# Attention with two MLP layers on one core: earlier weight conversions and an earlier x split in the first batch

## The chip, the cores and the metric

The kernel runs on one core of one Trainium2 chip. The metric is the device time of one execution in microseconds (us); lower is better. The engines are PE (TensorE, matmuls and transposes), DVE (VectorE), ACT (ScalarE) and POOL (GpSimd). SP issues nearly all DMAs of this kernel, from a queue that works in order.

## The reference

Attention over 4 batches, 8 heads, 576 positions and a head dimension of 64, with a threshold below each row's maximum, and after it two MLP layers (512 to 2048 to 512) with different activations. All in float32:

```python
scores = (q @ k.T) / sqrt(64)
scores = where(scores >= max(scores) - tau, scores, -1e9)
attn = exp(scores - max(scores)); attn = attn / (sum(attn) + 1e-9)
x = (attn @ v), heads side by side          # 2304 x 512
h = x @ w_in1
g = where(h >= 1, h, where(h <= -1, 0, (h + 1)**2 / 4))
x = g @ w_out1
h = x @ w_in2
out = (h * clip(h + 3, 0, 6) / 6) @ w_out2
```

## The kernel before, in words

**Attention.** The heads are taken two at a time: 16 jobs, four to a batch. A job has five blocks of query rows (four of 128, one of 64). Each block computes scores on PE (line 335), which DVE copies out of PSUM with the row maxima (line 348); ACT takes the exponent (line 360), DVE applies the threshold and sums (lines 363 and 369), PE transposes the result (line 284), ACT copies it out (lines 397 to 415), and PE multiplies by v (line 433). From job 4 on, q and k come in strips of 32 columns (line 227, from SP), and DVE transposes them (lines 293 and 309). When a job is done, its rows are divided by their sums: for most jobs POOL multiplies with factors that take a way through DRAM (lines 452 to 488); in the last job of the first batch PE transposes the factors and DVE multiplies (lines 496 to 507).

`attention()` is a generator that writes the blocks out one after the other, with the blocks' counter `t` from 0 (`mode["t"]` counts from 1). What has to happen beside a block is entered in `plan` by `at(t, what, j)`: "q" and "k" load and turn the next job, "z", "f" and "n" are the steps of the division. Job j's "n" stands at t = 5j + 9.

**First layer.** As soon as the four jobs of batch 0 are done, `dense1` starts on its rows, in groups of 256 columns, and runs between the blocks of the later jobs (PE lines 676 and 738). Every float32 operand is taken apart into a rounded part and the rest, and a product is made of three matmuls. `split_x` does this for x, in four pieces of 128 rows, one to a job (`kk`): ACT writes the rounded part (line 656), DVE the rest (line 657). Where x is still in SBUF (`here`), the pieces are read from there.

**Weights.** They are converted item by item, 512 KB each, in two halves. `split_a` has lines 118 and 121 on ACT, 122 on POOL, 129 on DVE; `split_b` has 135 on DVE, 137 on POOL, 139 on ACT and 141 on POOL. Five raw buffers stand in turn; after each second half the next load is issued from SP (lines 96 and 99). During the first batch halves are written by the loop at the end of the program, at most one to a block, until FIRST = 5 items are converted; after that `pace` writes them by the progress of `dense1`.

**Order.** The instructions are reordered when the program is built: an instruction that is ready may be put ahead of where it is written. `after(...)` holds some in place: the ACT lines 118 and 139 come behind the last exponent that was written before them, and in `split_x` line 656 behind the last exponent, line 657 behind the last mask.

Of the kernel before, what the change touches and what calls it, by code (L numbers as in the profile page):

```python
# [18 lines left out]
def kernel(  # L19
# [17 lines left out]
    KD = DM // 128  # L37
# [33 lines left out]
    def narrow(t, g):  # L71
        return t[g // 2][:, :, (g % 2) * GRP:(g % 2 + 1) * GRP]

    def f32(ap):
        return ap.bitcast(F32)
# [109 lines left out]
    weights = Weights()  # L185
# [5 lines left out]
    NBLK = 5  # L191
# [15 lines left out]
    mode = {"mlp": False, "att": True, "step": False, "t": 0, "s": 0, "n": 0}  # L207
# [233 lines left out]
    def pv_run(n):  # L441
        for _ in range(min(n, len(pvq))):
            pv_chunk()
# [68 lines left out]
    def attention():  # L512

        order = [(j, i) for j in range(NJ) for i in range(NBLK)]
        n = len(order)
        turns, tailq, maskq = [], [], []
        plan = {}

        def at(t, what, *x):
            plan.setdefault((t, what), []).append(x)  # L520

        for j in range(NJ):
            at(NBLK * j + (4 if j < HP - 1 else 3), "q", j + 1)
            at(NBLK * j + 4, "k", j + 1)
            at(NBLK * j + NBLK + 0, "z", j)
            at(NBLK * j + NBLK + 1, "f", j)
            at(NBLK * j + NBLK + 4, "n", j)

        def now_at(what):
            return plan.get((t, what), [])  # L530

        def masked():
            while maskq:
                b = maskq.pop(0)
                em_mask(*b)
                turns.append(b)
                tailq.append(b)

        def due(lag):
            r = []  # L540
            while turns and (len(turns) > lag or t >= n):
                r.append(turns.pop(0))
            return r

        def tails(lag):
            while tailq and (len(tailq) > lag or t >= n):
                em_tail(*tailq.pop(0))

        for t in range(n + 6):
            mode["t"] += 1  # L550
            mode["step"] = True
            if not mode["mlp"]:
                if t < n:
                    em_scores(*order[t])
                    maskq.append(order[t])
                pv_run(2)
                yield
                if t < n:
                    em_exp(*order[t], 0)
                    em_exp(*order[t], 1)  # L560
                masked()
                for x in now_at("z"):
                    pre_norm(*x)
                for x in now_at("f"):
                    fetch_norm(*x)
                yield
                now = due(1)
                for b in now:
                    em_pt(*b, 0)
                    yield  # L570
                for x in now_at("q"):
                    unit_q(*x)
                    yield
                for b in now:
                    if b[1] < NBLK - 1:
                        em_pt(*b, 1)
                        yield
                for b in now:
                    if b[1] in AFTER:
                        pvq.extend((b[0], AFTER[b[1]], c) for c in range(5))  # L580
                pv_run(3)
                for x in now_at("k"):
                    unit_k(*x)
                    yield
                tails(1)
                for x in now_at("n"):
                    em_norm(*x)
                    yield
            else:
                if t < n:  # L590
                    em_scores(*order[t])
                    maskq.append(order[t])
                    em_exp(*order[t], 0)
                    em_exp(*order[t], 1)
                for x in now_at("z"):
                    pre_norm(*x)
                for x in now_at("f"):
                    fetch_norm(*x)
                masked()
                yield  # L600
                for x in now_at("n"):
                    em_norm(*x)
                    yield
                now = due(1)
                tails(1)
                pv_run(5)
                yield
                for x in now_at("q"):
                    unit_q(*x)
                    yield  # L610
                for b in now:
                    em_pt(*b, 0)
                    yield
                pv_run(5)
                for b in now:
                    if b[1] < NBLK - 1:
                        em_pt(*b, 1)
                        yield
                for x in now_at("k"):
                    unit_k(*x)  # L620
                    yield
                for b in now:
                    if b[1] in AFTER:
                        pvq.extend((b[0], AFTER[b[1]], c) for c in range(5))


    xs, gs, acc, cnt = {}, {}, {}, {"h": 0, "a": 0}
# [3 lines left out]
    def split_x(key, kks=range(KD)):  # L631
        m, g, ph = key[:3]
        r = xs.setdefault(key, [])
        for kk in kks:
            if kk < len(r):
                continue
            b = g // 2 if ph == 1 else g
            if ph == 1:
                pool, n, bufs = mt, GRP, 1
                if all(b * HP + x in here for x in (kk, kk | 1)):  # L640
                    src = here[b * HP + kk][:, (g % 2) * GRP:(g % 2 + 1) * GRP]
                else:
                    if kk % 2 == 0:
                        t = mt.tile([128, 2, GRP], F32, tag="io", name="xst", bufs=2)
                        nc.sync.dma_start(out=t, in_=narrow(xd, g)[:, kk:kk + 2, :])
                    src = t[:, kk % 2]
            elif ph == 2 and g == NB - 1:
                pool, n, bufs = wide["x"], MAIN, 2
                src = here[b * HP + kk][:, 0:MAIN]
            else:  # L650
                pool, n, bufs = wide["x"], WIDE[g], 2
                src = wide["p"].tile([128, n], F32, tag="xst", name="xst", bufs=3)
                nc.sync.dma_start(out=src, in_=(x2d if m == 1 else xd)[g][:, kk, :])
            hi = pool.tile([128, n], F32R, tag=f"xh{kk}", name="xh", bufs=bufs)
            lo = pool.tile([128, n], F32R, tag=f"xl{kk}", name="xl", bufs=bufs)
            x = S.activation(out=hi, in_=src, func=ACTF.Copy)
            y = V.tensor_tensor(out=lo, in0=src, in1=f32(hi), op=ALU.subtract)  # L657
            if mode["att"]:
                after(x, pins["S"])
                after(y, pins["M"])  # L660
            r.append((hi, lo))
# [148 lines left out]
    def round_key(r):  # L810
        return (0, ROUNDS[r][0], 1, r)

    def dense1(ready, ahead):

        for n, l in enumerate(steps[:n_h]):
            r, f = hs[n]
            key = round_key(r)
            if key not in xs:
                while not ready(key[1]):
                    yield None  # L820
                split_x(key)
            ahead(n, f)
            yield from em_h(key, 0, f)
            if f == ROUNDS[r][1][-1]:
                xs.pop(key)
                if r + 1 < len(ROUNDS) and ready(ROUNDS[r + 1][0]):
                    split_x(round_key(r + 1))
            if n == n_h - 3 and not mode["att"]:
                split_x((0, NB - 1, 2))
            yield 0.33  # L830
            for i, (r, half, f) in enumerate(l):
                if i == 1:
                    pace(n + 0.5)
                yield from em_part(round_key(r), half, f)
                yield 0.33
# [102 lines left out]
    FIRST, RATE = 5, 0.85  # L938
    credit = 0.0
    for _ in attention():  # L940
        if not mode["mlp"]:
            if mode["t"] == 3:
                weights.prefetch()
            if mode["t"] >= 5 and mode["step"]:
                mode["step"] = False
                if weights.done < FIRST and mode["t"] % 5 in (0, 4):
                    weights.half()
            if not ready(0):
                continue
            mode["mlp"] = True  # L950
        credit = min(credit + share, 3.0)
        while credit > 0:
            c = next(part1)
            if c is None:
                break
            credit -= c
# [95 lines left out]
```

## Time and profile before

| | |
|---|---|
| Median of 3 runs | 1119.1 us (1118.22 to 1119.16) |
| Profiled execution | 1118.67 us, span 1116.9 us |
| Mean granted clock of PE | 0.992 |
| Busy, share of the span | PE 97%, PEld 79%, DVE 52%, ACT 55%, POOL 39% |
| Instructions | 17595 |

The span is the time from the first to the last instruction of the profiled execution. Busy time is a share over stages with different limits, so each stage has to be read by itself. A granted clock of 1.00 is 2.4 GHz, one of 0.50 is 1.2 GHz.

### The profile page before, as it was taken

What the parts mean: (1) busy time and instruction counts of PE and PEld (TensorE: products, weight loads), DVE (VectorE), ACT (ScalarE), POOL (GpSimd) and SP (SyncE); (2) the same over time, 40 slices, a digit from 0 to 9 for tenths busy, and PEclk for the clock granted to TensorE, in tenths of its full rate; (3) what the DMA queues carried; (4) which work ended last, traced back from release to release, by engine and by line L of the source; (5) the groups of instructions that cost most, each with busy time, mean ns of one, the idle gap of its engine ahead of it and who ended that gap; (6) DMA issues with size and microseconds to landing.
All of it is one profiled execution on the core that took longest, in us unless ns stands there. A gap on an engine that the chain in (4) does not pass through costs nothing.

```text
span 1116.9 us, 17595 instructions
## 1 busy us (share of the span) xinstructions
PE 1087.4 (97%) x6478; PEld 882.1 (79%) x6478; DVE 583.3 (52%) x1204; ACT 614.0 (55%) x1215; POOL 438.4 (39%) x382
## 2 busy tenths in 40 slices
PE   7998889999999999999999999999999999999998
PEld 5555667777878877888889888888888888898886
DVE  5899887876666656355536765558411111211111
ACT  5777886866667666556557766555432222333222
POOL 0233767622222111155627566567522222222221
PEclk9999889999999999999999999999999999999999
DMA  6454445433222110025222544533010110010001
GB/s 165 118 100 107 124 120 150 103 93 74 63 59 62 43 43 22 12 67 170 77 94 78 157 143 145 158 114 111 24 38 1 33 38 1 10 38 8 13 1 38
DMA packets 140230, 84.26 MB, mean 75 GB/s; under 512 B 99440, under 2 KB 123248, under 8 KB 140144
## 3 DMA queue, kind: packets, MB, share of 16 engines
q1 hardware_dynamic: 138800, 82.84, 27.0%
q8 instruction: 51, 0.84, 0.3%
q10 hardware_dynamic: 1344, 0.30, 0.1%
q14 instruction: 35, 0.29, 0.1%
HBM read 65.73 MB, written 17.37 MB: 74 GB/s over the span
## 4 chain that ended last, share of the span: by engine, by line
PE 88%; DVE 7%; ACT 2%; POOL 1%; issue 1%; SPq 1%; DMA 0%; DVEq 0%; POOLq 0%; ACTq 0%
PE Q L676 35%; PE P L718 28%; PE Q L738 7%; PE Q L433 6%; PE P L335 6%; PE Q L284 5%; DVE p L348 2%; DVE p L369 2%; ACT e L360 1%; DVE xl L657 1%; SPq L227 0%; PE Q L904 0%; DVE th L363 0%; DVE w_c L135 0%; DMA w_raw<-in_moe_w_out_dram 0%
## 5 line engine op out<-in xcount | busy, mean ns | idle before, releaser
L694 POOL TENSOR_TENSOR gl<-r,gh 128x512 fp32r<-128x512 f32 (+1 forms) x190 | 202.6, 1067 | 501.0 <-ACT gh L693 500.5
L676 PE MATMUL Q<-xh,wih 128*128 128x512 f32 (+1 forms) x760 | 262.0, 345 | 0.9 <-DVE r L687 0.7
L676 PE MATMUL Q<-xl,wih 128*128 128x512 f32 (+1 forms) x760 | 257.1, 338 | 0.0
L676 PE MATMUL Q<-xh,wil 128*128 128x512 f32 (+1 forms) x760 | 256.8, 338 | 0.0
L690 DVE SCALAR_TENSOR_TENSOR r<-r,Q 128x512 f32<-128x512 f32 (+1 forms) x80 | 50.7, 633 | 249.4 <-ACT r L689 249.3
L693 ACT ACTIVATE gh<-r 128x512 fp32r<-128x512 f32 (+1 forms) x190 | 99.9, 526 | 125.3 <-PE P L718 53.2
L676 PEld LDWEIGHTS Q<-xh,wih 128*128 128x128 f32 x760 | 144.1, 190 | 24.3 <-issue 4.2
L676 PEld LDWEIGHTS Q<-xl,wih 128*128 128x128 f32 x760 | 144.2, 190 | 16.0
L676 PEld LDWEIGHTS Q<-xh,wil 128*128 128x128 f32 x760 | 144.0, 190 | 15.5
L348 DVE TENSOR_SCALAR_CACHE_REDUCE p<-P 128x576 f32<-128x576 f32 x144 | 104.0, 751 | 53.3 <-PE Q L284 41.0
L369 DVE SCALAR_TENSOR_TENSOR p<-p,th,e 128x576 f32<-128x576 f32 x144 | 122.8, 873 | 15.1 <-ACT e L360 9.5
L689 ACT ACTIVATE r<-Q,three 128x512 f32<-128x512 f32 (+1 forms) x80 | 51.4, 643 | 142.9 <-PE Q L676 138.3
L360 ACT ACTIVATE e<-p,nm 128x576 f32<-128x576 f32 x144 | 108.9, 775 | 34.5 <-DVE p L348 33.6
L687 DVE SCALAR_TENSOR_TENSOR r<-r,Q 128x256 f32<-128x256 f32 (+1 forms) x110 | 54.8, 498 | 125.7 <-ACT r L686 122.4
L284 PE MATMUL Q<-ident,p 128*128 128x128 f32 x656 | 107.9, 282 | 9.8 <-ACT Gf L397 6.5
L718 PE MATMUL P<-woh,gh 128*128 128x512 f32 x288 | 111.9, 390 | 0.6 <-DVE ob L776 0.6
L718 PE MATMUL P<-wol,gh 128*128 128x512 f32 x288 | 112.2, 390 | 0.0
L718 PE MATMUL P<-woh,gl 128*128 128x512 f32 x288 | 111.0, 390 | 0.0
L335 PE MATMUL P<-kt,qt 64*128 64x288 f32 (+1 forms) x640 | 99.5, 429 | 11.0 <-DVE p L348 9.0
L284 PEld LDWEIGHTS Q<-ident,p 128*128 128x128 f32 x656 | 73.6, 141 | 46.3 <-ACT Gf L397 14.0
L137 POOL TENSOR_TENSOR w_c<-w_c,w_raw 128x512 int32<-128x512 int32 x64 | 89.5, 1400 | 41.3 <-DVE w_c L135 23.0
L397 ACT ACTIVATE Gf<-Q 128x512 f32<-128x512 f32 x128 | 74.4, 596 | 33.5 <-PE Q L284 32.8
(91 smaller groups left out, 1840.1 us busy)
## 6 DMA issues: line engine op xcount, KB each, us to landing
w_raw<-in_moe_w_in_dram SPq DMA_DIRECT2D x32, 512.0 KB
w_raw<-in_moe_w_out_dram SPq DMA_DIRECT2D x32, 512.0 KB
vn<-in_v_dram SPq DMA_DIRECT2D x32, 128.0 KB
x2p<-ob SPq DMA_DIRECT2D x16, 256.0 KB
x2d<-ob SPq DMA_DIRECT2D x16, 256.0 KB
xst<-x2d SPq DMA_DIRECT2D x16, 256.0 KB
out_dram<-ob SPq DMA_DIRECT2D x16, 256.0 KB
xst<-xd SPq DMA_DIRECT2D x15, 256.0 KB
```

Source lines behind the costliest of these rows:

```text
L137: x = G.tensor_tensor(out=c.bitcast(I32), in0=c.bitcast(I32), in1=r, op=ALU.add)
L284: x = T.transpose(out, in_, ident)
L335: mm = T.matmul(o, qt[j][r, c], kt[j][r, k0:k0 + HS], start=True, stop=True, skip_group_check=True)
L348: reads(V.tensor_scalar(out=p[:, x], in0=s[:, :, 0:HS], scalar1=-1.0, scalar2=3e38, op0=ALU.mult, op1=ALU.min, accum_out=nm[:, x:x + 1]), ...
L360: pins["S"] = S.activation(out=e, in_=p[:, x], func=ACTF.Exp, bias=nm[:, x:x + 1], scale=-1.0)
L369: pins["M"] = V.scalar_tensor_tensor(out=p[:, x], in0=p[:, x], scalar=th[:, x:x + 1], in1=e, op0=ALU.is_le, op1=ALU.mult, accum_out=zt[j][ ...
L397: S.activation(out=f[:, h, :, d0:d0 + 128], in_=tm.rearrange("p (c n) -> p c n", c=4), func=ACTF.Copy)
L676: mm = T.matmul(h, l[:, kk * 128:(kk + 1) * 128], r, start=(x == 0), stop=(x == 3 * KD - 1))
L693: x = S.activation(out=gh, in_=r, func=ACTF.Copy)
L694: y = G.tensor_tensor(out=gl, in0=r, in1=f32(gh), op=ALU.subtract)
L718: T.matmul(a, l, r, start=(first and x == 0), stop=(last and x == 2))
L738: mm = T.matmul(o, l, r, start=(f == fs[0] and x == 0 and i == 0), stop=(f == fs[-1] and x == 2 and i == 1), skip_group_check=True)
```

## The change

In the first batch a half of a conversion is written in blocks whose counter ends on 0, 2 or 4 modulo 5, instead of 0 or 4. And two of the four pieces of the first x split are written at t = 12 and t = 17 (jobs 0 and 1), three blocks after the division of their job; the other two stay where the first layer starts.

```diff
@@ attention(), the plan @@
             at(NBLK * j + NBLK + 4, "n", j)
+            if j < 2:
+                at(NBLK * j + NBLK + 7, "x", j)
@@ attention(), end of a block of the first batch @@
                 for x in now_at("n"):
                     em_norm(*x)
                     yield
+                for x in now_at("x"):
+                    split_x(round_key(0), range(x[0] + 1))
@@ dense1() @@
-            if key not in xs:
+            if len(xs.get(key, ())) < KD:
                 while not ready(key[1]):
                     yield None
                 split_x(key)
@@ the loop that drives attention @@
-                if weights.done < FIRST and mode["t"] % 5 in (0, 4):
+                if weights.done < FIRST and mode["t"] % 5 in (0, 2, 4):
                     weights.half()
```

## Rows read from the trace of the kernel before

**Rows 1.** The page's slices of the span, tenths of PE's busy time.

```profile
PE   7998889999999999999999999999999999999998
```

**Rows 2.** Busy time by stretches: PE, PEld, DVE, ACT, POOL, granted clock, DMA share, GB/s.

```profile
28.00:56.00 28.00, 27.06 (x194) 16.37 (x192) 24.08 (x67) 21.85 (x47) 6.30 (x5) 1.00 0.47 119
...
84.00:112.00 28.00, 22.72 (x164) 15.04 (x166) 26.85 (x72) 20.71 (x47) 10.12 (x9) 1.00 0.50 107
```

**Rows 3.** The same view in slices of 3 us.

```profile
87.00:90.00 3.00, 1.90 (x13) 1.24 (x13) 3.00 (x9) 2.74 (x8) 1.28 (x1) 1.00 0.78 128
...
111.00:114.00 3.00, 1.24 (x8) 0.69 (x8) 2.78 (x8) 3.00 (x6) 1.53 (x1) 0.82 0.60 187
114.00:117.00 3.00, 2.42 (x9) 1.19 (x11) 3.00 (x9) 2.69 (x7) 1.46 (x2) 0.50 0.16 50
```

**Rows 4.** Timeline from 111 us: start, duration, instruction, [idle before and its releaser].

```profile
111.54 1.24 PE L335 MATMUL P<-kt,qt 64*128 64x288 f32 x8 [2.15 <-DVE p L348]
...
114.58 0.45 PE L284 MATMUL Q<-ident,p 128*128 128x128 f32 x1 [1.80 <-DVE p L369]
...
123.23 0.42 DVE L687 SCALAR_TENSOR_TENSOR r<-r,Q 128x256 f32<-128x256 f32 x1 [2.08 <-ACT r L686]
```

**Rows 5.** The chain of waits in order of time: start, duration, what.

```profile
82.37 0.58 ACT w_raw L118
82.95 0.57 ACT w_c L121
...
90.18 2.84 PE Q L433 x20
...
106.89 1.01 DVE xl L657 x3
107.90 0.60 DVE w_c L135
...
108.83 1.17 DVE z L452
...
115.02 5.20 PE Q L433 x20
...
133.10 3.86 DMA w_raw<-in_moe_w_out_dram
...
149.01 2.13 PE Q L676 x12
...
157.12 1.43 PE Q L676 x12
```

**Rows 6.** Timelines of DVE, ACT and POOL in the first batch.

```profile
27.19 0.69 DVE L135 SCALAR_TENSOR_TENSOR w_c<-w_raw,w_c 128x512 uint32<-128x512 uint32 x1
27.79 0.16 DVE L452 TENSOR_SCALAR z<-z 128x9 f32<-128x9 f32 x1
...
39.65 1.30 DVE L369 SCALAR_TENSOR_TENSOR p<-p,th,e 128x576 f32<-128x576 f32 x1
...
44.62 0.42 DVE L129 TENSOR_SCALAR w_c<-w_c 128x512 uint32<-128x512 uint32 x1
45.73 0.82 DVE L369 SCALAR_TENSOR_TENSOR p<-p,th,e 128x576 f32<-128x576 f32 x1 [0.70 <-ACT e L360]
...
39.50 0.64 ACT L139 ACTIVATE wih<-w_c 128x512 fp32r<-128x512 f32 x1
...
40.29 1.79 POOL L141 TENSOR_TENSOR wil<-w_c,wih 128x512 fp32r<-128x512 f32 x1
```

**Rows 7.** Timelines of SP's queue, DVE and POOL in the first batch.

```profile
63.79 1.98 SPq L227 DMA_DIRECT2D qn<-in_q_dram  x4
...
67.64 0.78 DVE L293 STREAM_TRANSPOSE qt<-qn 128x576 f32<-128x576 f32 x1 [0.50 <-DMA qn<-in_q_dram]
...
27.96 1.28 POOL L137 TENSOR_TENSOR w_c<-w_c,w_raw 128x512 int32<-128x512 int32 x1 [2.89 <-DVE z L452]
...
99.40 1.38 POOL L141 TENSOR_TENSOR wil<-w_c,wih 128x512 fp32r<-128x512 f32 x1 [7.59 <-ACT wih L139]
```

## The prediction

> **What bounds the kernel now.** I read the page's slices first: from the seventh on (168 us) PE is at nine tenths or more to the end, so nothing that only frees another engine there can shorten the run [rows 1]. Then the busy times by stretch. What this change can win or lose lies before that, where the first batch of attention runs (to about 104 us) and the first layer starts. In the first batch no engine stands alone: from 28 to 56 us PE is busy for 27.06 of 28 us and DVE for 24.08; from 84 to 112 us it is DVE (26.85) that is full, and PE has 5.3 us of holes [rows 2].
>
> Third, slices of 3 us around the start of the first layer, where the granted clock leaves its full level: 0.82 in the slice from 111 us and 0.50 (1.2 instead of 2.4 GHz) in the next [rows 3]. Ahead of that PE had stood idle twice, 2.15 us for DVE's pass over the scores (L348) and 1.80 us for DVE's mask (L369) [rows 4]. Last, the chain of waits. From 106.89 to 110.04 it is DVE's queue and nothing else: three x splits, the vector part of a weight conversion (L135), one more split, then z (L452), behind which the score pass stands that PE waits for [rows 5]. A little later the same twenty L433 matmuls that take 2.84 us at full clock take 5.20 us, and DVE is then idle for 2.08 us before L687 because PE comes late [rows 4, 5].
>
> **The change, part by part.** I number blocks as the kernel's counter does (five to a job; block 25 is the last before the first layer). Before, conversion halves are written in blocks 5, 9, 10, 14, 15, 19, 20, 24, 25, and a tenth when the layer starts. After, they stand in 5, 7, 9, 10, 12, 14, 15, 17, 19, 20: all five conversions are written five blocks earlier, and none is left for the start of the layer. A first half issues L118, L121 (ACT), L122 (POOL), L129 (DVE); a second one L135 (DVE), L137 (POOL), L139 (ACT), L141 (POOL), and after it one 512 KB load goes to SP's queue.
>
> Where an operation is written is not where it runs. The second half written in block 9 has its L139 at 39.50 us, but its L135 already at 27.19 us, in a hole of DVE [rows 6]: the program is reordered when it is built, and only L139, pinned behind an exponent, and L141 after it stay. So a half that moves costs DVE something only where its operation no longer finds a hole.
>
> Job 1 (blocks 6 to 10). The L129 written in block 10 (0.42 us) stood in front of a wait of 0.70 us for ACT's exponent [rows 6]; in block 9 DVE has no hole: +0.42. Its L118 and L121 leave the queue ahead of that exponent, which is worth between nothing and the 0.70 us of waiting. I take half, −0.35. L135 can take the hole that is left: 0. Together +0.07.
>
> Job 2 (blocks 11 to 15). New here are L129 in block 12, L135 near block 14 and one x split's vector part: 0.42 + 0.69 + 0.34 (a third of 1.01) = 1.45 us of DVE [rows 5, 6]. DVE and PE are both near full at this point, so it costs between 0 and 1.45. Nothing says which of the two engines it meets, and I take half, +0.73.
>
> Job 3 (blocks 16 to 20). The second x split adds 0.34. In block 20 the chain passes through L118 and L121, 0.58 + 0.57 us [rows 5]; afterwards an L139 of 0.64 [rows 6] stands there: −0.51. Together −0.17.
>
> POOL. Before 104 us there will be one L137 and one L141 more than now. Beside the L141 at 40.29 the DVE mask took 1.30 us, against 0.82 for one with nothing beside it [rows 6]; I charge this 0.48 for each of the two, +0.96. The lower bound is 0. The upper one is that DVE stands still for both. The Trainium skill (SBUF — State Buffer, section "Who interferes with whom") states that upper end as a rule: GpSimd and a VectorE instruction of certain kinds hold a shared port pair for the whole instruction, and the other one waits. That speaks against the change, and is a rival below.
>
> ACT also runs the two early x splits; the 6 us in 28 in which it is idle hide them [rows 2]. Without that cover they cost what their vector parts do, twice 0.34. The splits read x where it lies, so they issue no DMA, and the product that they wait for is written three blocks earlier.
>
> SP. Of the five 512 KB loads that follow the conversions the first stays, as its L137 already ran early, and the other four go out earlier. SP's queue in job 2 is free up to the strips of the next q and k at 63.79 [rows 7]; I cost this at nothing, covered by that gap. If the cover is gone, strips stand behind a load, and DVE's transposes behind the strips: up to 3.86 us, the one load that shows on the chain [rows 5].
>
> Start of the layer. From DVE's queue L129 (0.42), L135 (0.60) and two of four x splits (0.67) disappear. L452 took 1.17 us on the chain while an L137 ran beside it, and 0.16 us elsewhere [rows 5, 6]; the L137 is gone too: −1.01. Together −2.70, all on the chain. What is late next is the mask (L369) at 112.89, for which PE still stands idle for 1.80 us [rows 4].
>
> Clock. With 2.70 us less on DVE the first of PE's two gaps closes, so it is likely that the clock stays at full level. The chain then loses 5.20 − 2.84 = 2.36 us, of which DVE, full meanwhile, can use only its 2.08 us of idle time. I take 2.08; lower bound 0.
>
> Sum: 0.07 + 0.73 − 0.17 + 0.96 = +1.59 before the layer, −2.70 at its start, −2.08 by the clock: **−3.19 us**. The profiled execution took 1118.67 us (span 1116.9 and 1.8 around it), 0.4 below the median of the runs. 1118.67 − 3.19 = 1115.5, or **1115.9** against the median of 1119.1. What is won by 125 us is kept, since the work after it is the same.
>
> **The rivals.** *The clock falls anyway.* For it: the 1.80 us gap stays, and other gaps only move. Against it: the slice from 87 us, with PE busy for 1.90 us of 3, kept the full clock [rows 3]. Then the sum is 1.59 − 2.70 = −1.11: 1118.0.
>
> *POOL holds DVE for whole instructions.* The extra L137 and L141 then cost 1.28 + 1.38 us, 2.66 instead of 0.96 (both from the trace's POOL rows in the first batch [rows 7]). The sum becomes −1.49: 1117.6. Against it: beside a POOL operation the masks grew by 0.48 us, not by the whole of it. This is the case in which the page named above would decide.
>
> *Earlier loads hold up the strips: slower.* Place: SP's queue from 63.79 us, where the chain passes through strip issues. A load that waits on SP for its buffer, or fills the rings just ahead of the strips, delays q and k of job 4 by up to 3.86 us; PE then stands idle long enough for the clock to fall in the first batch, 2.36 us more. 3.86 + 2.36 − 3.19 = +3.03: 1122.1. It decides once the strips come over 2 us late, as a gap of 2.15 us was followed by a fall [rows 3, 4]. Against it: DVE now waits 0.50 us for q there [rows 7], so something of a delay is already in.
>
> *More falls of the clock go too.* Two more slow stretches follow. Twelve L676 matmuls in the first of them took 2.13 us against 1.43 [rows 5], so each is worth between 0.70 and 2.08 us; both at the middle, 2.8. −3.19 − 2.8 = −6.0: 1113.1. For it: DVE and POOL would come into these stretches with less backlog. Against it: conversions from the sixth on are written as before.
>
> That the edit does little, because the build floats operations wherever holes are, is part of the first rival: only ACT's and POOL's pinned parts are sure to move.
>
> **How the numbers follow.** Forecast 0.42, clock falls anyway 0.22, POOL 0.08, loads 0.16, more falls go 0.12. About 0.2%, or 2.2 us, is what a measurement here can tell from no change: faster means below 1116.9. The forecast's own halves and bounds spread it from 1113.9 to 1118, some 0.30 of its 0.42 below the line; with the last rival and edges of the others faster has 0.46. Same takes the rest of the forecast and most of the first two rivals, 0.35. Slower has the loads and a few hundredths of the first rival, 0.19. The range is 1112.6 to 1121.2: it leaves out the far side of the loads' case and the low edge of the last one.
>
> **What would show it.** Right: no w_c or second-half operations between 100 and 112 us; two x splits there instead of four; z near 0.2 us; no granted clock of 0.50 between 111 and 120; the layer's first matmuls no later than now. Wrong: the first layer starts over 2 us later than at 107 us (then the first batch paid more than 1.59); a wait for q or k strips longer than 0.5 us near 67; or a slice at half clock before 104 us. If PE's idle time up to 200 us shrinks and the end doesn't come earlier, the work after 125 us gave it back, and the last step fails.

## The result and the profile after

| | before | after |
|---|---|---|
| Median | 1119.13 us (4 runs) | 1130.7 us (4 runs, 1127.88 to 1131.41) |
| Ratio, 95% interval | 1 | 1.0103 [1.009, 1.0116] |
| Profiled execution, span | 1118.67 us, 1116.9 us | 1131.17 us, 1129.4 us |

The kernel became slower by 11.6 us; 1115.9 had been forecast, and the range ended at 1121.2. The profiled executions differ by 12.5 us.

The first look goes to the stretches. Busy times of PE, PEld, DVE, ACT and POOL, granted clock, DMA share and GB/s, before:

```profile
0.00:104.00 104.00, 92.54 (x649) 59.10 (x650) 84.56 (x230) 75.02 (x151) 26.01 (x34) 1.00 0.52 123
104.00:130.00 26.00, 19.48 (x124) 13.09 (x125) 22.99 (x56) 20.19 (x45) 15.21 (x12) 0.87 0.50 132
130.00:240.00 110.00, 102.59 (x751) 80.74 (x749) 92.92 (x206) 85.03 (x189) 73.87 (x63) 0.95 0.47 116
240.00:1100.00 860.00, 859.98 (x4908) 719.27 (x4905) 380.48 (x713) 430.64 (x829) 320.71 (x271) 1.00 0.22 63
```

And after:

```profile
0.00:104.00 104.00, 88.50 (x602) 56.09 (x602) 83.22 (x218) 73.17 (x145) 27.81 (x36) 0.97 0.53 128
104.00:130.00 26.00, 19.94 (x145) 13.00 (x142) 24.25 (x59) 20.20 (x44) 9.80 (x9) 0.97 0.41 95
130.00:240.00 110.00, 94.32 (x678) 73.16 (x679) 93.02 (x194) 80.31 (x176) 69.58 (x61) 0.95 0.42 112
240.00:1100.00 860.00, 859.85 (x4949) 719.50 (x4949) 387.08 (x730) 435.18 (x843) 323.39 (x273) 1.00 0.22 64
```

From 240 us PE is full in both, so what it does less before then is what the kernel ends later by. Up to 104 us it is busy for 4.04 us less and loses some at a clock of 0.97; from 104 to 130 it wins 0.46 and the clock is better, 0.97 instead of 0.87; from 130 to 240 it is busy for 8.27 us less. Together that is 214.61 − 202.76 = 11.85 of the 12.5 us.

The same can be followed by the first score pass (L348) of a block. Against before it comes 6.15 us later in block 25, 1.09 us *earlier* in block 28, 5.04 later in block 31 and 12.25 later in block 46, and the distance then stays to the end. (Job 0 begins 0.80 us earlier in the trace of after, so what the first batch lost by block 25 is 6.95.) So between blocks 25 and 28, where the layer starts, the changed kernel gains some 7 us by this marker, and what lies on both sides took 19. Part of the gain is work that only moved: between these two markers PE does 26 of the layer's matmuls (L676) and 29 transposes (L284) before, and 13 (L680) and 24 after. From the chain's rows (1.43 us for twelve L676, 1.13 for nine L284) I estimate this at 13 × 0.119 + 5 × 0.126 = 2.2 us, which leaves a gain of about 5.0. From block 25 to block 46 both kernels do the same of the layer (240 matmuls of L676 or L680, 176 of L738 or L742), so the 12.25 us there are all loss.

**The start of the layer** is as forecast. DVE's timeline after:

```profile
111.87 0.82 DVE L369 SCALAR_TENSOR_TENSOR p<-p,th,e 128x576 f32<-128x576 f32 x1
...
112.62 0.76 DVE L661 TENSOR_TENSOR xl<-xu,xh 128x256 fp32r<-128x256 f32 x2
113.29 0.17 DVE L452 TENSOR_SCALAR z<-z 128x9 f32<-128x9 f32 x1
...
114.12 0.76 DVE L348 TENSOR_SCALAR_CACHE_REDUCE p<-P 128x576 f32<-128x576 f32 x1 [0.17 <-PE P L335]
```

Two splits in place of four, z at 0.17 instead of 1.17, and no conversion in between [rows 5]. The clock is kept, where it was 0.82 and 0.50 [rows 3], and the chain passes through the twenty L433 in 2.84 instead of 5.20 us [rows 5]. The slices, and behind them the line of the chain:

```profile
111.00:114.00 3.00, 2.06 (x14) 1.46 (x14) 2.84 (x10) 1.36 (x4) 0.97 (x1) 1.00 0.87 190
114.00:117.00 3.00, 2.79 (x21) 2.02 (x19) 2.50 (x7) 2.39 (x6) 0.00 (x0) 1.00 0.35 58
```

```profile
118.45 2.84 PE Q L433 x20
```

**The first batch.** DVE's groups up to 104 us: busy time and mean ns of one, then idle time before. Before:

```profile
L369 DVE SCALAR_TENSOR_TENSOR p<-p,th,e 128x576 f32<-128x576 f32 x44 | 36.5, 851 | 4.2 <-ACT e L360 2.1
...
L363 DVE TENSOR_SCALAR th<-nm,taus 128x2 f32<-128x2 f32 x20 | 5.7, 286 | 0.7
...
L135 DVE SCALAR_TENSOR_TENSOR w_c<-w_raw,w_c 128x512 uint32<-128x512 uint32 x4 | 2.7, 684 | 0.0
...
L129 DVE TENSOR_SCALAR w_c<-w_c 128x512 uint32<-128x512 uint32 x4 | 1.7, 426 | 0.0
```

After:

```profile
L369 DVE SCALAR_TENSOR_TENSOR p<-p,th,e 128x576 f32<-128x576 f32 x41 | 36.5, 911 | 4.0 <-ACT e L360 2.2
...
L363 DVE TENSOR_SCALAR th<-nm,taus 128x2 f32<-128x2 f32 x19 | 6.8, 359 | 0.6
L135 DVE SCALAR_TENSOR_TENSOR w_c<-w_raw,w_c 128x512 uint32<-128x512 uint32 x5 | 3.5, 710 | 0.0
...
L129 DVE TENSOR_SCALAR w_c<-w_c 128x512 uint32<-128x512 uint32 x5 | 2.1, 420 | 0.0
...
L661 DVE TENSOR_TENSOR xl<-xu,xh 128x256 fp32r<-128x256 f32 x2 | 0.8, 418 | 0.0
```

In the same 36.5 us DVE gets through three masks less. Longer masks cost 41 × 0.060 = 2.5 us, longer thresholds 19 × 0.073 = 1.4, the operations that are new here 0.8 + 0.4 + 0.8 = 2.0: 5.9 us in sum, of which the shorter z (L452) gives back 0.6. And PE's clock falls, as it did not in any slice here before:

```profile
90.00:93.00 3.00, 1.68 (x7) 1.38 (x9) 3.00 (x10) 2.21 (x5) 1.16 (x2) 0.63 0.69 107
93.00:96.00 3.00, 3.00 (x14) 1.63 (x14) 2.04 (x7) 0.78 (x4) 2.40 (x3) 0.50 0.80 206
```

What comes ahead of that fall, in the timelines of POOL, DVE and PE:

```profile
89.27 1.28 POOL L137 TENSOR_TENSOR w_c<-w_c,w_raw 128x512 int32<-128x512 int32 x1
...
89.58 1.59 DVE L369 SCALAR_TENSOR_TENSOR p<-p,th,e 128x576 f32<-128x576 f32 x1
...
91.33 1.30 PE L284 MATMUL Q<-ident,p 128*128 128x128 f32 x5 [2.52 <-ACT wih L139]
```

The mask begins 0.31 us after POOL's L137 and takes 1.59 instead of 0.82 us; PE's transposes read what it writes and begin 0.16 us after its end at 91.17. (The profile names ACT's L139 as the releaser, which ended at 91.22. In `h_only` and `pin_x1`, shown further below, the transposes begin 0.16 us after the mask's end too, at a time when no L139 ends; so I take the mask for what they waited for.)

**After the start of the layer** the same happens on a larger scale:

```profile
123.77 1.24 DVE L129 TENSOR_SCALAR w_c<-w_c 128x512 uint32<-128x512 uint32 x1
...
125.61 1.22 DVE L135 SCALAR_TENSOR_TENSOR w_c<-w_raw,w_c 128x512 uint32<-128x512 uint32 x1
...
127.07 1.74 DVE L369 SCALAR_TENSOR_TENSOR p<-p,th,e 128x576 f32<-128x576 f32 x1
...
128.74 1.81 DVE L369 SCALAR_TENSOR_TENSOR p<-p,th,e 128x576 f32<-128x576 f32 x1
...
126.90 1.29 POOL L137 TENSOR_TENSOR w_c<-w_c,w_raw 128x512 int32<-128x512 int32 x1 [0.63 <-DVE w_c L135]
128.27 1.67 POOL L141 TENSOR_TENSOR wil<-w_c,wih 128x512 fp32r<-128x512 f32 x1
129.90 1.77 POOL L141 TENSOR_TENSOR wol<-w_c,woh 128x512 fp32r<-128x512 f32 x1
...
131.29 2.18 PE L335 MATMUL P<-kt,qt 64*64 64x288 f32 x8 [4.31 <-DVE p L348]
```

Two conversions run together: two L129 and two L135 begin within 5 us on DVE (the second of each is shown), then on POOL L137, L141 and L141 with hardly a hole, and both masks beside them take double. PE stands for 4.31 us, and the clock is at 0.50 in the slice from 129 us. Before, there were such masks too, of 1.53 us at 112.89 and 1.83 at 118.39, but no two of them one behind the other. And there the first L137 of that time was followed on POOL by the next conversion's L122 and only then by the L141: the conversions took turns. The order in which the build laid POOL's instructions shows the same. With a for L122, b for L137, c for L141 and the other letters for other work, it was `..agbancgbacbqgacgbacb..` from the start of the layer, and is now `..aagbnbccqgaagbbccg..`: two conversions side by side, though not a line that writes them there was changed. By group from 112 to 170 us, DVE's L135 went from a mean of 680 to 1095 ns and L129 from 548 to 817 (below).

### The profile page after: what moved, and what is told of

The parts are those of the page before. It is cut to its first block, busy times and chain, and to the rows that moved or that the text cites. A ratio compares the mean times of both kernels' runs of the same rounds, so it can differ in the third digit from the quotient of the medians.

```text
span 1129.4 us, 17600 instructions
## 1 busy us (share of the span) xinstructions
PE 1087.9 (96%) x6478; PEld 882.0 (78%) x6478; DVE 591.6 (52%) x1204; ACT 615.3 (54%) x1215; POOL 435.7 (39%) x382
## 4 chain that ended last, share of the span: by engine, by line
PE 85%; DVE 7%; ACT 3%; POOL 2%; DMA 1%; issue 1%; SPq 0%; DVEq 0%; POOLq 0%; ACTq 0%
PE Q L680 33%; PE P L722 27%; PE Q L742 7%; PE P L335 6%; PE Q L433 6%; PE Q L284 5%; DVE p L369 2%; DVE p L348 2%; ACT e L360 1%; DVE w_c L135 1%; POOL w_c L137 1%; DVE xl L661 1%; DMA w_raw<-in_moe_w_in_dram 1%; DVE w_c L129 0%; DMA vn<-in_v_dram 0%
## 5 line engine op out<-in xcount | busy, mean ns | idle before, releaser
L680 PE MATMUL Q<-xh,wih 128*128 128x512 f32 (+1 forms) x760 | 262.1, 345 | 3.0 <-DVE r L691 1.7
L680 PE MATMUL Q<-xl,wih 128*128 128x512 f32 (+1 forms) x760 | 257.0, 338 | 0.0
L680 PE MATMUL Q<-xh,wil 128*128 128x512 f32 (+1 forms) x760 | 257.0, 338 | 0.0
L680 PEld LDWEIGHTS Q<-xh,wih 128*128 128x128 f32 x760 | 144.1, 190 | 26.1 <-issue 4.6
L680 PEld LDWEIGHTS Q<-xl,wih 128*128 128x128 f32 x760 | 144.1, 190 | 15.7
L680 PEld LDWEIGHTS Q<-xh,wil 128*128 128x128 f32 x760 | 144.0, 190 | 15.4
L369 DVE SCALAR_TENSOR_TENSOR p<-p,th,e 128x576 f32<-128x576 f32 x144 | 127.2, 902 | 15.9 <-ACT e L360 10.2
L348 DVE TENSOR_SCALAR_CACHE_REDUCE p<-P 128x576 f32<-128x576 f32 x144 | 104.2, 752 | 55.3 <-PE Q L284 37.7
L284 PE MATMUL Q<-ident,p 128*128 128x128 f32 x656 | 109.9, 285 | 18.2 <-ACT Gf L397 7.2
L691 DVE SCALAR_TENSOR_TENSOR r<-r,Q 128x256 f32<-128x256 f32 (+1 forms) x110 | 54.9, 499 | 124.3 <-ACT r L690 119.1
L284 PEld LDWEIGHTS Q<-ident,p 128*128 128x128 f32 x656 | 75.1, 143 | 56.5 <-issue 14.8
L137 POOL TENSOR_TENSOR w_c<-w_c,w_raw 128x512 int32<-128x512 int32 x64 | 87.3, 1365 | 37.4 <-DVE w_c L135 22.0
```

Source lines behind the costliest of these rows:

```text
L137: x = G.tensor_tensor(out=c.bitcast(I32), in0=c.bitcast(I32), in1=r, op=ALU.add)
L284: x = T.transpose(out, in_, ident)
L348: reads(V.tensor_scalar(out=p[:, x], in0=s[:, :, 0:HS], scalar1=-1.0, scalar2=3e38, op0=ALU.mult, op1=ALU.min, accum_out=nm[:, x:x + 1]), ...
L369: pins["M"] = V.scalar_tensor_tensor(out=p[:, x], in0=p[:, x], scalar=th[:, x:x + 1], in1=e, op0=ALU.is_le, op1=ALU.mult, accum_out=zt[j][ ...
L680: mm = T.matmul(h, l[:, kk * 128:(kk + 1) * 128], r, start=(x == 0), stop=(x == 3 * KD - 1))
```

## The experiments

Medians are of four to ten runs, ratios against runs of the kernel before on the same chip.

### Each part alone, and two small moves

`h_only` leaves the early x split out, `x_only` the added half, `shift_03` moves one half of a job in the kernel before, and `nine` is the changed kernel with a tenth half left for the start of the layer, as before.

```diff
# h_only: the diff without its first three hunks; x_only: the diff without its last hunk
# shift_03, on the kernel before
-                if weights.done < FIRST and mode["t"] % 5 in (0, 4):
+                if weights.done < FIRST and mode["t"] % 5 in (0, 3):
# nine, on the changed kernel
-                if weights.done < FIRST and mode["t"] % 5 in (0, 2, 4):
+                if 2 * weights.done + weights.mid < 9 and mode["t"] % 5 in (0, 2, 4):
```

> Halves in three of five blocks, x split at once as before. Theory 'halves' (the loss of 11.6 us comes from conversions crowding DVE, ACT and POOL in the first batch, where the clock fell at 91 us): 1127 to 1133 us. Theory 'x split' (it comes from the two split pieces): 1116 to 1120. Theory 'order' (both loss and gain come from how the build interleaves the instructions of jobs 5 to 7, which any shift of a few instructions changes): anything from 1112 to 1133, and the two parts alone do not add up to +11.6.

> Two pieces of the x split early, halves in two of five blocks as before. 'Halves': 1116 to 1120 us. 'x split': 1127 to 1133. 'Order': anything from 1112 to 1133, with the sum of the two parts more than 3 us away from +11.6.

> The kernel before, with the second half of each conversion written one block earlier (counter modulo 5 in 0 or 3 instead of 0 or 4): the same number of halves before the first layer, no x split early. 'Halves' and 'x split' both expect no change, 1117 to 1121 us, as nothing is added to the first batch. 'Order' expects a move of more than 2.2 us in some direction.

> The changed kernel, but the tenth half is left to the start of the first layer as before. 'Halves': between 1124 and 1131 us, as one half of six that moved is back. 'x split': 1127 to 1133, unchanged. 'Order': more than 3 us away from the changed kernel's 1130.7.

| | median us | ratio | block 25, 28, 31, 46 against before, us |
|---|---|---|---|
| after | 1130.7 | 1.0103 [1.009, 1.0116] | +6.15, −1.09, +5.04, +12.25 |
| h_only | 1125.84 | 1.0066 [1.005, 1.0083] | +2.11, −5.16, +1.34, +6.26 |
| x_only | 1126.97 | 1.0076 [1.0058, 1.0095] | +1.26, −2.89, +1.61, +8.02 |
| shift_03 | 1118.6 | 1.0001 [0.9992, 1.001] | |
| nine | 1130.59 | 1.0104 [1.0086, 1.0122] | |

Either part alone makes the kernel slower, by 7.5 and 8.6 us, though each is ahead at block 28, by 5.16 and 2.89 us, some of it work that moved behind this marker, as above. At block 31 both are behind again. What is common to them is the order afterwards: POOL's conversions run in pairs in both. `shift_03`, the one edit of the four behind which the order at and after the start of the layer came out unchanged, costs nothing. `nine` says that the tenth half is not what matters. The theory 'order' fits the two parts, whose losses add up to 16.1 and not to 11.6 us; it missed in `shift_03`, which was to move by more than 2.2 us, and in `nine`, which was to lie over 3 us from 1130.7. The clock is not what costs the parts their time: from 130 to 240 us their granted clock is 0.98, above the 0.95 of before, and yet PE is busy there for 96.36 (`h_only`) and 93.77 us (`x_only`) instead of 102.59.

The parts also tell who stretches the masks of the first batch. Their mean up to 88 us (ahead of any fall of the clock) is 855 ns before, 901 after, 903 in `h_only` and 864 in `x_only`: it is the added halves, not the splits. And neither part alone has the fall of the clock at 91 us. In `h_only` the mask comes first and POOL second:

```profile
88.77 0.81 DVE L369 SCALAR_TENSOR_TENSOR p<-p,th,e 128x576 f32<-128x576 f32 x1
...
88.89 1.84 POOL L137 TENSOR_TENSOR w_c<-w_c,w_raw 128x512 int32<-128x512 int32 x1
...
89.74 0.74 PE L284 MATMUL Q<-ident,p 128*128 128x128 f32 x5 [1.59 <-ACT e L360]
```

Here the mask takes 0.81 us and POOL's L137 1.84 instead of 1.28, the mirror image of the case above. PE stands for 1.59 us instead of 2.52, and the clock stays.

### The conversions made to take turns again

If the pairing costs time, a pin that forbids it must give some back. The pin puts a conversion's first POOL operation (L122) behind the L137 of the conversion ahead of it. It restores the alternation; in the kernel before, where L122 and L137 alternate anyway, it changes nothing of the program that is built. It was put on the changed kernel and on both parts; `after_ser` has instead ACT's first operation (L118) behind the L139 of the conversion ahead, so that two conversions don't overlap on ACT.

```diff
# after_pin, h_pin, x_pin
-            G.tensor_scalar(
-                out=f32(c), in0=f32(c), scalar1=122879.9921875, scalar2=2.0 ** -15, op0=ALU.min, op1=ALU.max)
+            after(G.tensor_scalar(out=f32(c), in0=f32(c), scalar1=122879.9921875, scalar2=2.0 ** -15,
+                                  op0=ALU.min, op1=ALU.max), pins.get("W"))
# split_b, behind L137
-        after(x, pins["G"])
+        after(x, pins["G"]); pins["W"] = x
# after_ser: L118 after(x, pins.get("W")), and pins["W"] = x behind L139
```

> The changed kernel with one more pin: L122 of a conversion comes on POOL behind L137 of the conversion before it, as it does by itself in the kernel before. In the changed kernel the conversions after the layer's start run two by two (L122 L122, L137 L137, L141 L141), and DVE's L135 beside them takes 1.1 instead of 0.68 us. Theory 'pairs' (that is the common loss of about 7 us between 120 and 170 us): 1121 to 1125 us, the mean of L135 there back near 0.7 us, PE's loss from 120 to 170 us within 2 us of the kernel before's 8.1. Theory 'earlier start' (the layer that starts earlier meets work that is not ready, whatever the order of conversions): 1128 to 1132 us.

> Halves alone, with the same pin. 'Pairs': 1116 to 1121 us, 5 us or more below the 1125.8 without it. 'Earlier start': 1124 to 1128.

> The early x split alone, with the same pin. 'Pairs': 1116 to 1121 us, 5 us or more below the 1127.0 without it. 'Earlier start': 1125 to 1129.

> The changed kernel with a stricter pin: ACT's L118 of a conversion comes behind L139 of the one before, so that no two conversions overlap on ACT at all. 'Pairs': no collision of two conversions is left, so at or below the run with the weaker pin, 1119 to 1125 us, unless the longer way of each conversion makes the weights late. 'Earlier start': 1128 to 1133.

Measured: `after_pin` 1125.49, 1.0065 [1.005, 1.008]; `h_pin` 1124.25, 1.0046 [1.003, 1.0063]; `x_pin` 1124.05, 1.0049 [1.0034, 1.0064]; `after_ser` 1125.49, 1.006 [1.0045, 1.0075]. The pin gives back 5.2 us of the changed kernel by the medians (4.8 by what each lies above the kernel before on its own chip), and its interval lies clear of the old one. It gives back 1.6 and 2.9 us of the parts, where the intervals overlap and the theory 'pairs' had asked for 5 or more. DVE's groups from 112 to 170 us show where. Before, after, and with the pin:

```profile
L369 DVE SCALAR_TENSOR_TENSOR p<-p,th,e 128x576 f32<-128x576 f32 x18 | 18.1, 1023 | 0.7 <-ACT e L360 0.5
...
L135 DVE SCALAR_TENSOR_TENSOR w_c<-w_raw,w_c 128x512 uint32<-128x512 uint32 x8 | 5.4, 680 | 0.0
...
L129 DVE TENSOR_SCALAR w_c<-w_c 128x512 uint32<-128x512 uint32 x8 | 4.4, 548 | 0.5 <-POOL w_c L122 0.5
```

```profile
L369 DVE SCALAR_TENSOR_TENSOR p<-p,th,e 128x576 f32<-128x576 f32 x17 | 19.4, 1151 | 2.0 <-ACT e L360 1.6
...
L135 DVE SCALAR_TENSOR_TENSOR w_c<-w_raw,w_c 128x512 uint32<-128x512 uint32 x7 | 7.7, 1095 | 0.0
...
L129 DVE TENSOR_SCALAR w_c<-w_c 128x512 uint32<-128x512 uint32 x7 | 5.7, 817 | 0.5 <-POOL w_c L122 0.5
```

```profile
L369 DVE SCALAR_TENSOR_TENSOR p<-p,th,e 128x576 f32<-128x576 f32 x18 | 19.9, 1116 | 4.2 <-ACT e L360 3.7
...
L135 DVE SCALAR_TENSOR_TENSOR w_c<-w_raw,w_c 128x512 uint32<-128x512 uint32 x7 | 5.7, 821 | 0.0
...
L129 DVE TENSOR_SCALAR w_c<-w_c 128x512 uint32<-128x512 uint32 x7 | 4.0, 570 | 0.0
```

By count times difference of the means, the changed order costs DVE 17 × 0.128 + 7 × 0.415 + 7 × 0.269 = 7.0 us in this stretch, and with the pin 18 × 0.093 + 7 × 0.141 + 7 × 0.022 = 2.8. The 4.2 us between them are near the 5.2 that the pin gives. The parts don't bear this out in size: by the same count the pin frees 4.4 us of DVE in `h_only` and 4.1 in `x_only`, and the runs gain 1.6 and 2.9. So an order without pairs is worth about 5 us to the changed kernel, but the pin makes the order of the other work anew as well, and how much of the 5 us belongs to the pairs alone is not shown. Pairing is not the only cause either: `after_ser` has masks of 1035 ns here, near the 1023 of before, and ends no earlier than `after_pin`.

`nine` speaks against the pairs as the whole explanation. After one pair its conversions take turns on POOL from 129 to 170 us, and yet it takes 1130.59 us, and its seven L135 from 112 to 170 us have a mean of 1276 ns. Three of them begin right behind an L141 of the conversion ahead:

```profile
137.91 1.46 POOL L141 TENSOR_TENSOR wol<-w_c,woh 128x512 fp32r<-128x512 f32 x1
138.28 1.64 DVE L135 SCALAR_TENSOR_TENSOR w_c<-w_raw,w_c 128x512 uint32<-128x512 uint32 x1
```

So what stretches DVE's operation is that it begins just behind one of POOL's; a pair is one order that brings this about, and there are others.

### Other neighbours of both kernels

What remains, 5 to 7 us, could be a price of early work, or what any other order than the tuned one costs. So the kernel before was moved the other way (`late8`: the first half one block later, eight instead of nine halves in the batch), and the two constants were moved that say how much of the layer runs between attention's blocks (`share`) and how fast conversions follow (`RATE`).

```diff
# late8, on the kernel before
-            if mode["t"] >= 5 and mode["step"]:
+            if mode["t"] >= 6 and mode["step"]:
# before_s55, and pin_s55 on after_pin
-    share = 0.57
+    share = 0.55
# before_r90
-    FIRST, RATE = 5, 0.85
+    FIRST, RATE = 5, 0.9
```

> The kernel before, changed the other way: eight halves before the first layer instead of nine, so that the whole fifth conversion falls on the layer's start; no x split early. Theory 'chosen order' (the kernel before stands at an order of jobs 5 to 8 that is several us better than its neighbours, and any edit near the layer's start, in either direction, loses it): 1121 to 1130 us, and here the conversions run in pairs as well. Theory 'more early is bad' (the loss grows with the work moved ahead, so less of it ahead gains or changes nothing): 1115 to 1120 us.

> The kernel before with share 0.55 instead of 0.57: a little less of the first layer between the blocks, nothing moved in the first batch or at the layer's start. 'Chosen order': 1121 to 1128 us. 'More early is bad': 1117 to 1121 us.

> The kernel before with RATE 0.90 instead of 0.85: conversions a little earlier from the layer's fourth step on, the rest as before. 'Chosen order': 1120 to 1127 us. 'More early is bad': 1116 to 1120 us, as the layer's start is untouched.

> The changed kernel with the pin of after_pin and share 0.55. If the remaining 6.8 us of after_pin are the loss of a chosen order, its neighbours scatter around 1125 by a few us, 1120 to 1130, and this one can be on either side of it; if they are the price of the early work itself, it stays within 2.2 us of 1125.5.

Measured: `late8` 1126.05, 1.0067 [1.005, 1.0084]; `before_s55` 1120.93, 1.0025 [1.0015, 1.0035]; `before_r90` 1122.69, 1.0033 [1.002, 1.0047]; `pin_s55` 1126.11, 1.0071 [1.0056, 1.0086]. The edit in the opposite direction costs 7.8 us, as much as a part of the change, and in it too the conversions run in pairs from the start of the layer. So a cost of this size doesn't need earlier work; a later half brings it as well. `pin_s55` lies 0.6 us from `after_pin`, which both theories allow.

### The collision at 91 us, and a last try for the rest

`pin_x1` is `after_pin` with the early split of job 0 alone. In it the mask near 90 us and POOL's L137 change places by a hair. `late8_pin` puts the pin on `late8`. The other four look for a better order: `pin_r80` and `pin_r90` (RATE on `after_pin`), `hpin_r90` (RATE 0.9 on `h_pin`) and `xpin_s56` (share 0.56 on `x_pin`).

```diff
# pin_x1, on after_pin
-            if j < 2:
+            if j < 1:
                 at(NBLK * j + NBLK + 7, "x", j)
```

> after_pin with only one of the two early x pieces (job 0's). In the changed kernel the DVE mask at 89.58 us started 0.3 us after POOL's L137 and took 1.59 us, PE stood idle for 2.52 us and the clock fell at 91 us. With halves alone the mask started first, took 0.81 us, the gap was 1.59 us and the clock stayed. Theory 'collision' (the second piece's 0.42 us on DVE put the mask behind L137): the mask there about 0.8 us, the gap below 2 us, no fall of the clock before 104 us, block 25 about 3 us earlier than in after_pin (107.3), the whole at 1121 to 1125 us. Theory 'halves' (ten halves in the first batch are enough for the gap): a fall of the clock near 91 us as in after_pin, 1124 to 1127 us.

> The kernel with eight early halves (late8) and the pin that keeps conversions from running in pairs. If pairs cost by themselves, whichever edit brings them, this one is faster than late8 (1126.1) by 1.5 to 5 us, as the three pinned kernels were against theirs, and its L135 is back from about 1.1 to 0.7 to 0.9 us; if the pin's gain belonged to the early work, 1125 to 1128.

> after_pin with RATE 0.80. Theory 'chosen order': the kernels with early work scatter as the order of jobs 5 to 8 falls out, over a range that reaches below 1121, so of these four at least one is below 1121 us. Theory 'no use for early work' (what is won at the layer's start is not kept, and the early work costs by itself): all four between 1122 and 1130 us.

> after_pin with RATE 0.90: conversions a little earlier from the layer's fourth step on. 'Chosen order': anywhere from 1116 to 1128 us; 'no use for early work': 1122 to 1130.

> h_pin with RATE 0.90. 'Chosen order': anywhere from 1116 to 1128 us; 'no use for early work': 1122 to 1128.

> x_pin with share 0.56. 'Chosen order': anywhere from 1116 to 1128 us; 'no use for early work': 1121 to 1128, and as this one moves the least work ahead, the lowest of the four.

| | median us | ratio |
|---|---|---|
| pin_x1 | 1125.41 | 1.0055 [1.0039, 1.0071] |
| late8_pin | 1123.43 | 1.0042 [1.0026, 1.0059] |
| pin_r80 | 1125.71 | 1.0068 [1.0051, 1.0084] |
| pin_r90 | 1125.07 | 1.006 [1.0045, 1.0075] |
| hpin_r90 | 1122.35 | 1.0034 [1.0023, 1.0045] |
| xpin_s56 | 1130.0 | 1.0098 [1.0073, 1.0123] |

`after_pin` still has the mask of 1.59 us, the gap of 2.52 and the fall of the clock at 91 us. In `pin_x1` all three are gone:

```profile
89.78 0.81 DVE L369 SCALAR_TENSOR_TENSOR p<-p,th,e 128x576 f32<-128x576 f32 x1
...
89.91 1.84 POOL L137 TENSOR_TENSOR w_c<-w_c,w_raw 128x512 int32<-128x512 int32 x1
...
90.75 0.74 PE L284 MATMUL Q<-ident,p 128*128 128x128 f32 x5 [1.59 <-ACT e L360]
```

Block 25 comes at +3.12 instead of +4.88 us. The end gains nothing from it (1125.41 against 1125.49): at block 28 `pin_x1` is at −3.88 against −2.35, at block 46 at +7.45 against +6.77. So for the second time something won before the layer is not there at 240 us. The pin on `late8` gives back 2.6 us, the fourth gain in four uses, though here too the intervals overlap.

The theory that the remaining 5 to 7 us are only the loss of a chosen order asked for one neighbour of the changed kernel below 1121; the best is 1122.35. The theory that early work costs them gave `xpin_s56` 1121 to 1128 us and the lowest time of the four; it is the highest (1124.9 to 1131.3 in its four runs) and ends 6 us above `x_pin`. Neither stands as it was put. No version tried beats the kernel before.

What the traces show of the rest is a place. PE's idle time from 130 to 240 us, 110 less its busy time, is 7.4 us before, 15.7 after and 11.3 to 11.5 in `after_pin`, `h_pin` and `pin_x1`. In these three, 3.4 to 3.9 us of it stand ahead of the layer's first product (L680, in `h_pin` L676), which waits for DVE's step of the activation (L691, L687) of the group ahead; before it was 0.9. Why the build arrives at such an order, and whether another one keeps the early work without it, stays open.

## Why the prediction was wrong

- **What bounds the kernel, and the start of the layer: right.** Two splits instead of four, z at 0.17, the clock kept, 2.84 for 5.20 us. The forecast charged −2.70 − 2.08 = −4.78 us; between blocks 25 and 28 the changed kernel wins 6.15 + 1.09 = 7.2 us by the marker, `h_only` 7.3 and `x_only` 4.2. Of the 7.2, about 2.2 are work that moved behind block 28, which leaves 5.0, close to the forecast. One reading was off without harm: the forecast put two idle times of PE ahead of the fall of the clock, but the trace has the fall at 112.92 us, when the second (1.80 us, from 112.78) had just begun.
- **"+1.59 before the layer": mis-sized.** It measured 6.95 us. The step that failed is the charge for POOL, 0.48 us for each of two operations. It was taken from one mask of 1.30 us beside one L141 and put on the added operations only, and it was read off the wrong neighbour. That mask began at 39.65 us, ahead of the L141 (40.29) and behind an L488 that the rows of before don't show (it stands below this list). It lost 0.48 us to the 0.69 that were left of L488; the L141, second behind the mask, took 1.79 instead of 1.28. So 0.48 is not what an operation costs, but what this order cost. Besides, the added operations also push the others to new places, so that 41 masks lost 2.5 us and the thresholds (L363), which had no term at all, 1.4. By block 25, each counted from its own job 0, `h_only` loses 2.80 us and `x_only` 1.32; the 2.8 that are missing to 6.95 come with the fall of the clock at 91 us, which only both parts together have. And "a slice at half clock before 104 us" stood on the list of what would show it wrong: it came, and the rival of the loads had priced such a fall at 2.36 us. Its cause was another than that rival's, though: DVE waits for no strip up to 104 us after, where it had waited 0.50 us before [rows 7]. It was a mask behind an L137, as `h_only` and `pin_x1` bear out, where the mask comes first and the clock stays.
- **The rival in which POOL holds DVE for whole instructions** was right in its mechanism, and priced in the wrong place. It was given 2.66 us in the first batch, for two operations. The Trainium skill (SBUF — State Buffer, section "Who interferes with whom") states that whoever issues first has the shared ports for the whole instruction, and that the order decides who waits. The trace agrees: mask second, 1.59 instead of 0.81 us; L137 second, 1.84 instead of 1.28. The second one is stretched by 0.77 and 0.56 us, somewhat less than what was left of the first at its start (0.97 and 0.69). Of the 144 masks in each trace, 124 before and 121 after began with POOL free or ahead of its operation, and none of these took more than 0.82 us. So the forecast's objection, that masks grew by 0.48 and not by the whole, fails: 0.48 was about what was left.
- **"What is won by 125 us is kept, since the work after it is the same": this step failed**, and most of the loss lies here: against before, the changed kernel goes from 1.09 us ahead at block 28 (about 1 behind, once the moved work is counted) to 12.25 behind at block 46. The work is the same, but not its order. The forecast said itself that the program is reordered when it is built, and used that only where operations move into holes ahead of the layer. From 130 to 240 us PE lost 8.27 us of busy time. About 5 us of the whole loss come back when conversions are kept from running in pairs, the pairs' own share of it not being shown; the rest is placed but not explained.
- **The clock falls anyway, and more falls go:** neither. The fall at 112.9 us is gone, and there are new ones, at 90.8 and 128.4, the first within the gap of 2.52 us, the second within that of 4.31. The two later slow stretches are not gone but elsewhere, and from 130 to 240 us the granted clock is 0.95 in both kernels.

The L488 of the kernel before, from POOL's timeline:

```profile
38.92 1.42 POOL L488 TENSOR_TENSOR xu<-xu,rb 128x576 f32<-128x576 f32 x1 [9.68 <-ACT Gf L397]
```

## What to carry to other kernels

Where the build makes the order anew, an edit is judged by the order of every engine behind it and not by the lines that it moves: compare the sequence of POOL's and DVE's instructions before and after ahead of any sum, and pin what the tuned order depends on. Time won ahead of a stretch in which several engines limit each other is not yet won at the end; follow one marker, such as the first score pass of each block, until it moves no more, and count the work between two markers, as work that moves behind one looks like a gain. The elementwise work on POOL was not free here beside DVE operations with two inputs in SBUF: its price was set by which of them started first, and in the first batch PE's clock paid as well.

## What was not expected of the hardware

- A DVE mask of 128x576 takes 0.82 us alone and 1.59, 1.74 and 1.81 beside POOL's L137 and L141; DVE's integer step on a 128x512 tile (L129) takes 0.42 alone and 1.24 beside L137. The stretch falls on the second of the two: POOL's L137 takes 1.28 first and 1.84 second, and no mask that began ahead of POOL's operation took more than 0.82.
- Within PE gaps of 2.52 and 4.31 us the granted clock fell from 2.4 to 1.2 GHz; with one of 1.59 us in the place of the first it did not. In the fall at 91 us the chain's twenty L433 take 3.72 us instead of 2.84.
- One constant moved by 2 to 6%, which changes nothing but the order in which the work is written, moved the time by 0.2 to 6 us (`pin_r80` against `after_pin`, `xpin_s56` against `x_pin`), though PE is full from 240 us on in each kernel of which the stretches are shown here.
